# ELU with its exponential in the free half of h's PSUM bank, masks built in three steps, range check behind the last ELU

## The chip, the cores and the metric

The kernel runs on one core of one Trainium2 chip. The core has a matrix engine (TensorE, PE in the profile), a vector engine (VectorE, DVE), an activation engine (ScalarE, ACT), a general engine (GpSimd, POOL), and a queue engine (SyncE, SP) which here issues every transfer to 16 DMA engines. Each engine works through its own instructions in a fixed order and waits on semaphores for the others. The metric is the device time of one execution in microseconds. A profiled execution also has a span, from the first instruction to the last, which is a little shorter than its time.

## The reference

Attention with sink keys and a sliding window, then a two-layer network with an ELU between the layers:

```python
scores = scale * np.matmul(q, k.transpose(0, 1, 3, 2))       # 4 x 8 heads, 768 x 768, head_dim 64
keep = is_sink | in_window                                   # first n_sink=4 keys, or 0 <= rel < window=128
scores = np.where(keep, scores, -1000000000.0)
a = np.exp(scores - np.max(scores, axis=-1, keepdims=True))
x = np.matmul(a / (np.sum(a, axis=-1, keepdims=True) + 1e-09), v)
h = x @ w_in                                                 # 3072 x 512 by 512 x 2048
g = np.where(h > 0.0, h, alpha * (np.exp(np.minimum(h, 0.0)) - 1.0))
return (g @ w_out).astype(np.float32)                        # 2048 x 512
```

The weights come as 64-bit floats, everything else as 32-bit floats.

## The kernel before

The 24 tiles of 128 tokens are grouped into nine chunks of 2, 2, 2, 3, 3, 3, 3, 3 and 3 tiles (`SIZES`). For each chunk the attention goes through four pairs of heads, and in each pair through the chunk's tiles. Scores are made on PE (L540, L541, L547) into one of two PSUM banks `s`. DVE adds a mask and takes the row extreme (L566, one instruction for each head), ACT takes the exponential (L568), ACT and DVE write a high and a low half-precision part of the probabilities into `pq` (L580, L581), SP transposes `pq` into `pt` by DMA (L599), and PE multiplies by the values (L610, L615) into `po`, from which `x` is taken (L623, L624). There are three masks: `m0` for a sequence's first tile, `m1` for its second, `m2` for all others. `make_masks` builds `m0` and `m1` at once at the start, from `nw`, the two scalars that a DMA brings (`words`, L938 to L945), and returns `rest`, which builds `m2` and is an operation of the plan.

The feed-forward part takes 16 blocks of 128 hidden units, one after the other. A block `f` is 12 matmuls into one of two PSUM banks `h` (L651), the ELU, and three groups of matmuls into the accumulators `acc` (L672). The ELU is five operations: the exponential of `h` on ACT into the SBUF buffer `g` (L659), a subtraction and scaling of `g` in place on DVE (L661), the minimum with 0 and maximum with `h` on DVE (L662), a half-precision copy `gh` on ACT (L664), and the difference `gl` on POOL (L665). A bank holds 512 numbers a partition; a two-tile chunk uses 256 of them and a three-tile chunk 384. Chunks 0 and 1 go through the blocks in two halves each (`PARTS`), since the weights are still arriving: each of 32 weight pieces is loaded by SP (L395), put together from 64-bit words by one ACT and three DVE operations (L267 to L270), and split into two half-precision parts by ACT and POOL (L416, L417).

All of this is written as tasks of a `Plan`. PE's order is set by hand, by a position `pos`. The order on the other engines comes from a list scheduler: it gives each task a due time, counted back from PE's, and each engine takes, among the tasks that are ready by the plan's own costs (the second argument of `add`), the one that is due first. `keep_order` then writes the tasks in that order, and each engine keeps it. So a changed cost can move instructions on ACT, DVE, POOL and SP.

At the end `in_range` (L725 to L731) checks on DVE that the values stayed in range, a matmul with ones (L741) gathers this over the partitions, and `decide` (L735 to L737) makes a flag. Every engine loads the flag from SBUF (`TENSOR_LOAD`, L968) and jumps over a general path (L969) which isn't run here.

Of the kernel before, what the change touches and what calls it, by code (L numbers as in the profile page):

```python
# [280 lines left out]
def make_masks(nc, tmp, sk, nw, m0, m1, m2):  # L281
# [9 lines left out]
    nc.vector.tensor_scalar(sk, sk, nw[:, 0:1], None, ALU.is_lt)  # L291
# [7 lines left out]
    nc.vector.tensor_tensor(own, own, kp, ALU.mult)  # L299
# [4 lines left out]
    nc.gpsimd.memset(m0[:, 0:NS], MASKED)  # L304
# [1 line left out]
    for m in (m1, m2):
        nc.gpsimd.memset(m[:, KW : KW + NS], MASKED)
# [2 lines left out]
    nc.vector.tensor_copy(rel[:, 0:NS], kp[:, 0:NS])  # L310
    nc.vector.tensor_tensor(kp[:, 0:NS], kp[:, 0:NS], sk, ALU.max)
# [1 line left out]
    nc.gpsimd.memset(m1[:, 0:NS], MASKED)

    def rest():
        to_mask(m2[:, KW + NS : 2 * KW], own)
        nc.vector.tensor_copy(kp[:, 0:NS], rel[:, 0:NS])
        to_mask(m2[:, NS:KW], kp)
        to_mask(m2[:, 0:NS], sk)

    return rest


def fast_path(tc, ctx, first, kq, vx, wt, out, nw, flag):
# [672 lines left out]
```

## Time and profile before

| | before |
|---|---|
| time, median of 3 runs | 664.21 us (663.05 to 664.29) |
| time of the profiled execution | 662.14 us |
| its span | 660.3 us |
| busy share of the span: DVE, ACT, POOL | 69%, 69%, 51% |
| share of the chain that ended last: PE, DVE, ACT, POOL, DMA | 78%, 7%, 5%, 3%, 3% |
| mean granted PE clock | 0.984 |

The page gives busy times, and the chain of work that ended last, followed back from the last instruction. The tables by stretch of time give each engine's busy microseconds in a stretch, with the number of instructions in brackets, then the granted PE clock (1.00 is full), the DMA engines' busy share and the GB/s. In the tables of groups a row is a line, an engine, an operation and a form, then the count, the busy time and the mean ns of one, then the idle time of the engine ahead of these instructions and what ended it. In the order of time a row has the start, the length and the instruction, and in square brackets how long its engine was idle before it. An engine's name with a q behind it is its sequencer.

### The profile page before, as it was taken

To read this page: it belongs to the slowest core of one execution; us is meant where nothing else is said; L and a number is where in the kernel's file an instruction comes from. 1 tells how busy PE (TensorE), PEld (TensorE's weight loads), DVE (VectorE), ACT (ScalarE), POOL (GpSimd) and SP (SyncE) were. 2 spreads that over 40 slices of the span, in tenths; PEclk is the share of its full clock that TensorE was granted. 3 is DMA by queue.
4 is the path that set the end of the run, shared out by engine and by line. 5 is a ranking of instruction groups with operands and counts; after the bars stand their busy time and mean duration, and the time that the engine had idled before them with its cause. 6 is when DMAs were issued, how large, how long until landed. Compare 5 with 4: busy or idle time off the path is not lost.

```text
span 660.3 us, 13443 instructions
## 1 busy us (share of the span) xinstructions
PE 609.9 (92%) x4449; PEld 370.2 (56%) x4449; DVE 458.4 (69%) x1251; ACT 456.9 (69%) x1340; POOL 338.2 (51%) x497
## 2 busy tenths in 40 slices
PE   3486799789999999999999999999999999999996
PEld 2343466456776665555555556555555565555552
DVE  6999998896677776667677776758677787524222
ACT  4999786777788887767677777766677777523221
POOL 0158866785556666544555655444446564322221
PEclk9999698899999999999999999999999999999998
DMA  7989974857654586435454566555554734211001
GB/s 264 206 282 266 276 199 144 269 142 167 145 118 128 136 184 131 116 92 171 116 152 118 133 156 167 104 111 171 112 155 128 208 84 101 49 56 49 1 0 54
DMA packets 130110, 93.41 MB, mean 141 GB/s; under 512 B 104432, under 2 KB 109552, under 8 KB 130032
## 3 DMA queue, kind: packets, MB, share of 16 engines
q1 hardware_dynamic: 130032, 92.47, 53.2%
q8 instruction: 37, 0.61, 0.4%
q14 instruction: 41, 0.34, 0.2%
HBM read 59.94 MB, written 7.34 MB: 102 GB/s over the span
## 4 chain that ended last, share of the span: by engine, by line
PE 78%; DVE 7%; ACT 5%; issue 4%; POOL 3%; DMA 3%; SPq 0%; DVEq 0%; POOLq 0%; ACTq 0%
PE h L651 33%; PE acc L672 33%; PE po L610 5%; PE s L540 3%; PE s L541 3%; DMA pt<-pq 2%; PE s L547 1%; ACT e L568 1%; DVE wu L268 1%; POOL kq L487 1%; DVE wv L270 1%; DVE wu L269 1%; DVE pq L581 1%; DVE g L661 1%; POOL kq L489 1%
## 5 line engine op out<-in xcount | busy, mean ns | idle before, releaser
L651 PE MATMUL h<-x,w 128*128 128x384 f16 (+1 forms) x1728 | 276.6, 310 | 5.6 <-DVE g L662 5.6
L665 POOL TENSOR_TENSOR gl<-g,gh 128x384 f16<-128x384 f32 (+1 forms) x144 | 126.9, 882 | 215.2 <-ACT gh L664 184.4
L651 PEld LDWEIGHTS <-w 128*128 128x128 f16 x1728 | 165.6, 99 | 98.7 <-issue 5.9
L672 PE MATMUL acc<-w,gh 128*128 128x512 f16 x768 | 195.3, 384 | 0.8 <-DVE wv L693 0.8
L661 DVE TENSOR_SCALAR g<-g 128x384 f32<-128x384 f32 (+1 forms) x144 | 65.3, 454 | 115.8 <-ACT g L659 115.3
L659 ACT ACTIVATE g<-h 128x384 f32<-128x384 f32 (+1 forms) x144 | 64.9, 451 | 88.3 <-PE h L651 83.1
L581 DVE SCALAR_TENSOR_TENSOR pq<-e,st,pq 128x256 f16<-128x256 f32 (+1 forms) x192 | 107.2, 587 | 19.7 <-ACT pq L580 19.1
L672 PE MATMUL acc<-w,gl 128*128 128x512 f16 x384 | 110.6, 383 | 0.6 <-POOL gl L665 0.4
L672 PEld LDWEIGHTS <-gh 128*128 128x128 f16 x768 | 70.9, 98 | 71.5 <-issue 3.0
L568 ACT ACTIVATE e<-e,st 128x264 f32<-128x264 f32 (+1 forms) x192 | 93.4, 487 | 11.1 <-DVE st L566 9.7
L664 ACT ACTIVATE gh<-g 128x384 f16<-128x384 f32 (+1 forms) x144 | 69.3, 481 | 44.6 <-DVE g L662 44.2
L566 DVE CUSTOM_DVE_ANT_0 e<-s,m 128x264 f32<-128x264 f32 (+1 forms) x192 | 73.0, 404 | 32.1 <-PE s L541 26.8
L580 ACT ACTIVATE pq<-e,st 128x256 f16<-128x256 f32 (+1 forms) x192 | 85.1, 480 | 10.5 <-DVE st L573 10.1
L487 POOL TENSOR_TENSOR kq<-kqs,kq 128x396 fp32r<-128x396 f32 (+1 forms) x56 | 67.2, 1199 | 23.9 <-ACT kq L483 23.0
L662 DVE SCALAR_TENSOR_TENSOR g<-g,h 128x384 f32<-128x384 f32 (+1 forms) x144 | 72.6, 504 | 1.6
L672 PEld LDWEIGHTS <-gl 128*128 128x128 f16 x384 | 37.6, 99 | 47.9 <-POOL gl L665 2.5
L483 ACT ACTIVATE kq<-kqs 128x780 fp32r<-128x780 f32 (+2 forms) x56 | 48.4, 879 | 17.1 <-PE s L541 14.3
L417 POOL TENSOR_TENSOR w<-wv,w 128x512 f16<-128x512 f32 x32 | 39.5, 1236 | 38.8 <-ACT w L416 18.9
L489 POOL TENSOR_TENSOR kq<-kqs,kq 64x384 fp32r<-64x384 f32 (+1 forms) x56 | 56.7, 1013 | 4.4
L610 PE MATMUL po<-pt,vh 128*64 128x128 f16 x704 | 41.7, 230 | 17.8 <-DMA pt<-pq 7.8
L540 PE MATMUL s<-kq 128*128 128x264 f32 x160 | 56.2, 370 | 1.7 <-POOL kq L489 1.6
L610 PEld LDWEIGHTS <-vh 128*64 128x64 f16 x704 | 31.1, 115 | 29.6 <-issue 21.7
(78 smaller groups left out, 629.2 us busy)
## 6 DMA issues: line engine op xcount, KB each, us to landing
raw<-in_wt_dram SPq DMA_DIRECT2D x32, 512.0 KB, 5.6
kqs<-in_kq_dram SPq DMA_DIRECT2D x24, 456.0 KB, 3.4
kqs<-in_kq_dram SPq DMA_DIRECT2D x24, 390.0 KB, 3.3
out_dram<-wv SPq DMA_DIRECT2D x24, 256.0 KB, 2.5
vs<-in_vx_dram SPq DMA_DIRECT2D x20, 256.0 KB, 3.1
vm<-in_vx_dram SPq DMA_DIRECT2D x6, 768.0 KB, 4.6
kqs<-in_kq_dram SPq DMA_DIRECT2D x12, 326.0 KB, 4.1
vs<-in_vx_dram SPq DMA_DIRECT2D x12, 320.0 KB, 3.1
```

Of the source, the lines that this page charges most:

```text
L487: nc.gpsimd.tensor_tensor(buf[:, KQ_MAX : KQ_MAX + n] if c >= DUP else buf[:, kw : 2 * kw], raw[:, :n], hi[:, :n].bitcast(F32), ALU.subtract)
L540: nc.tensor.matmul(sp[:, :wd], q, hi[:, c0 : c0 + wd], start=True, stop=False)
L566: red = add("DVE", 0.13 + 0.00145 * wd, lambda ee=ee, me=me, sp=sps[e], m=m, wd=wd: nc.vector.tensor_tensor_reduce(ee, sp[:, :wd], m[:, :w ...
L568: ex = add("ACT", 0.48 + 0.00085 * wd, lambda ee=ee, me=me, rs=rs[:, e : e + 1]: nc.scalar.activation(ee, ee, AF.Exp, bias=me, scale=-1.0, ...
L580: a = add("ACT", act_us(nb * P, True), lambda src=src, hi=hi, re=re: nc.scalar.activation(hi, src, AF.Copy, scale=re), deps=[rr])
L581: b = add("DVE", dve_us(nb * P) + 0.1, lambda src=src, hi=hi, lo=lo, re=re: nc.vector.scalar_tensor_tensor(lo, src, re, hi, ALU.mult, ALU. ...
L610: nc.tensor.matmul(po[e * D : (e + 1) * D, oc], vv[:, vo : vo + D], pt[:, (2 * e + part) * nb + i, :], start=new, stop=last)
L651: nc.tensor.matmul(hp[:, :n], win[:, part, d, :], xx[:, :n], start=k == 0, stop=k == 3 * ND - 1)
L661: b = add("DVE", 0.1 + 0.0008 * n, lambda gf=gf: nc.vector.tensor_scalar(gf, gf, -1.0, G_SCALE, ALU.add, ALU.mult), deps=[a])
L662: b = add("DVE", dve_us(n), lambda gf=gf, hp=hp: nc.vector.scalar_tensor_tensor(gf, gf, 0.0, hp[:, :n], ALU.min, ALU.max), deps=[b])
L665: tl = add("POOL", pool_us(n), lambda gl=gl, gf=gf, gh=gh: nc.gpsimd.tensor_tensor(gl[:, :n], gf, gh[:, :n], ALU.subtract), deps=[th])
L672: nc.tensor.matmul(acc[i], gg[:, i * P : (i + 1) * P], wout[:, part, :], start=f == f0 and k == 0, stop=f == f1 - 1 and k == 2)
```

## The change

1. **ELU.** In chunks whose `h` uses at most half of its bank (chunks 0, 1 and 2: 48 of the 144 blocks), the exponential goes to the second half of the same bank, and the subtraction on DVE reads it there and writes `g` in SBUF. In three-tile chunks nothing moves.
2. **Masks.** `make_masks` is a generator. What needs no scalars stands ahead of them, `m0` follows at once, and `m1` and `m2` are operations of the plan (`mask1`, `mask2`). A product of two comparisons becomes one instruction, three copies go, and two four-column writes are added.
3. **Scalars.** The four comparisons and the reduction which test that `n_sink` and `window` are allowed become an operation of the plan (`allowed`) instead of standing ahead of the masks.
4. **Range check.** It also depends on the last block's L662, and its matmul stands behind PE's last accumulation instead of ahead of the last block's.
5. **Costs of the plan.** The exponential, the subtraction and POOL's split of the weights have other costs. `ON_ACT` is empty, so the weights' operations are the same.

```diff
 def make_masks(nc, tmp, sk, nw, m0, m1, m2):
...
     nc.vector.tensor_copy(rel, ri)
+    nc.vector.tensor_scalar(kp, rel, 0.0, None, ALU.is_ge)
...
+    for m in (m0, m1):
+        nc.gpsimd.memset(m[:, 0:NS], MASKED)
...
-    nc.vector.tensor_scalar(own, rel, nw[:, 1:2], None, ALU.is_lt)
-    nc.vector.tensor_scalar(kp, rel, 0.0, None, ALU.is_ge)
-    nc.vector.tensor_tensor(own, own, kp, ALU.mult)
-    nc.vector.tensor_copy(kp, own)
-    nc.vector.tensor_tensor(kp[:, 0:NS], kp[:, 0:NS], sk, ALU.max)
-    to_mask(m0[:, NS:KW], kp)
+    yield
+    nc.vector.tensor_scalar(sk, sk, nw[:, 0:1], None, ALU.is_lt)
+    nc.vector.scalar_tensor_tensor(own, rel, nw[:, 1:2], kp, ALU.is_lt, ALU.mult)
+    to_mask(m0[:, NS:KW], own)
+    nc.vector.tensor_tensor(kp[:, 0:NS], own[:, 0:NS], sk, ALU.max)
+    to_mask(m0[:, NS : 2 * NS], kp[:, 0:NS])
+    yield
     to_mask(m1[:, KW + NS : 2 * KW], own)
...
     nc.vector.tensor_scalar(kp, rel, float(P), nw[:, 1:2], ALU.add, ALU.is_lt)
-    nc.vector.tensor_copy(rel[:, 0:NS], kp[:, 0:NS])
-    nc.vector.tensor_tensor(kp[:, 0:NS], kp[:, 0:NS], sk, ALU.max)
     to_mask(m1[:, NS:KW], kp)
...
+    nc.vector.tensor_tensor(rel[:, 0:NS], kp[:, 0:NS], sk, ALU.max)
+    to_mask(m1[:, NS : 2 * NS], rel[:, 0:NS])
+    yield
+    to_mask(m2[:, KW + NS : 2 * KW], own)
+    to_mask(m2[:, NS:KW], kp)
+    to_mask(m2[:, 0:NS], sk)
+    yield
...
+    masks = make_masks(nc, tmp[:, : 4 * P], tmp[:, 4 * P : 4 * P + NS], nw, m0, m1, m2)
+    next(masks)
+    scalars()
+    next(masks)
...
-    rest_ = add("DVE", 0.9, rest)
+    mask1 = add("DVE", 1.0, lambda: next(masks))
+    mask2 = add("DVE", 0.6, lambda: next(masks), deps=[mask1])
+    allowed = add("DVE", 0.7, allowed)
...
-        tl = add("POOL", 1.5, lambda: nc.gpsimd.tensor_tensor(w[k][:, 1, :], v, w[k][:, 0, :], ALU.subtract), deps=[th])
+        tl = add("POOL", 1.22, lambda: nc.gpsimd.tensor_tensor(w[k][:, 1, :], v, w[k][:, 0, :], ALU.subtract), deps=[th])
...
-            a = add("ACT", act_us(n) + 0.06, lambda gf=gf, hp=hp, sums=sums: nc.scalar.activation(gf, hp[:, :n], AF.Exp, scale=1.0 / G_SCALE, accum_out=sums), deps=[s1])
+            ex = hp[:, n : 2 * n] if 2 * n <= 512 else gf
+            a = add("ACT", act_us(n) + 0.15, lambda ex=ex, hp=hp, sums=sums: nc.scalar.activation(ex, hp[:, :n], AF.Exp, scale=1.0 / G_SCALE, accum_out=sums), deps=[s1])
             exps_done.append(a)
-            b = add("DVE", 0.1 + 0.0008 * n, lambda gf=gf: nc.vector.tensor_scalar(gf, gf, -1.0, G_SCALE, ALU.add, ALU.mult), deps=[a])
+            b = add("DVE", 0.4 if 2 * n <= 512 else 0.45, lambda gf=gf, ex=ex: nc.vector.tensor_scalar(gf, ex, -1.0, G_SCALE, ALU.add, ALU.mult), deps=[a])
             b = add("DVE", dve_us(n), lambda gf=gf, hp=hp: nc.vector.scalar_tensor_tensor(gf, gf, 0.0, hp[:, :n], ALU.min, ALU.max), deps=[b])
             ring("h", [s1], [b])
+            g_done.append(b)
...
-    a = add("DVE", 2.0, in_range, deps=seen + exps_done)
-    b = add("PE", 0.1, lambda: nc.tensor.matmul(sp[:, 0:3], ones, some16, start=True, stop=True), deps=[a], pos=start + 2 * LAG - 1.5)
+    a = add("DVE", 2.0, in_range, deps=seen + exps_done + g_done[-1:] + [allowed])
+    b = add("PE", 0.1, lambda: nc.tensor.matmul(sp[:, 0:3], ones, some16, start=True, stop=True), deps=[a], pos=start + 2 * LAG)
```

PE's order is the same in the whole fast path, except for the check's matmul. On the other engines most of the order up to the third chunk differs in places. Three places matter below.

DVE at the start, from the scalars to the first masked scores (L566 before, L576 now, whose mask is the last name; `pt` is scratch space here, `m_172`, `m_173`, `m_174` before and `m_163`, `m_164`, `m_165` now are `m0`, `m1`, `m2`). Before, the last of 20 rows that stand between the scalars and the scores:

```order
L294 TENSOR_SCALAR m_173<-pt_108 128x128
L294 TENSOR_SCALAR m_174<-pt_108 128x128
L302 TENSOR_TENSOR pt_108<-pt_108 128x4
L294 TENSOR_SCALAR m_172<-pt_108 128x128
L309 TENSOR_SCALAR pt_108<-pt_108,words 128x128
L310 COPY pt_108<-pt_108 128x4
L311 TENSOR_TENSOR pt_108<-pt_108 128x4
L294 TENSOR_SCALAR m_173<-pt_108 128x128
L317 COPY pt_108<-pt_108 128x4
L294 TENSOR_SCALAR m_174<-pt_108 128x128
L294 TENSOR_SCALAR m_174<-pt_108 128x4
L566 ISA e_91,st_94<-s_166,m_172 128x132
```

Now, where ten rows stand there, the last of them:

```order
L303 TENSOR_SCALAR m_164<-pt_99 128x128
L303 TENSOR_SCALAR m_163<-pt_99 128x4
L317 TENSOR_SCALAR pt_99<-pt_99,words 128x128
L303 TENSOR_SCALAR m_164<-pt_99 128x128
L319 TENSOR_TENSOR pt_99<-pt_99 128x4
L303 TENSOR_SCALAR m_164<-pt_99 128x4
L576 ISA e_82,st_85<-s_157,m_163 128x132
L576 ISA st_85 128x1
L576 ISA e_82,st_85<-s_158,m_163 128x132
L576 ISA st_85 128x1
L303 TENSOR_SCALAR m_165<-pt_99 128x128 x2
L303 TENSOR_SCALAR m_165<-pt_99 128x4
```

The five operations of `allowed` and the three writes of `m2` no longer stand ahead of the first scores. `m2` is written right behind the first pair of them, and `allowed` stands some 300 rows further on.

DVE at the first block's ELU (`h` in PSUM, `g` in SBUF). Before:

```order
L573 RECIPROCAL st_96<-st_96 128x2
L661 TENSOR_SCALAR g_109<-g_109 128x256
L270 SCALAR_TENSOR_TENSOR wv_121<-acc_171,wu_125 128x512
L566 ISA e_92,st_98<-s_166,m_174 128x264
L566 ISA st_98 128x1
```

Now:

```order
L583 RECIPROCAL st_87<-st_87 128x2
L673 TENSOR_SCALAR g_100<-h_155 128x256
L271 TENSOR_SCALAR wu_115<-raw_117 128x512
L576 ISA e_83,st_89<-s_157,m_165 128x264
L576 ISA st_89 128x1
```

The source of the subtraction is now `h`'s bank, and another piece of the weights' work stands behind it.

DVE at the end, from the last block's subtraction to the jump (`checks` and `some` belong to the range check, `wv` is a tile of the result). Before:

```order
L729 TENSOR_REDUCE some<-checks 128x1
L730 TENSOR_SCALAR some<-some 128x2
L731 CAST some_204<-some 128x3
L662 SCALAR_TENSOR_TENSOR g_110<-g_110,h_165 128x384
L735 TENSOR_REDUCE some<-s_166 128x1
L736 TENSOR_SCALAR some<-some 128x1
L737 TENSOR_TENSOR words<-words,some 128x1
L967 CAST words<-words 128x1
L697 TENSOR_SCALAR wv_121<-acc_169 128x512
L697 TENSOR_SCALAR wv_123<-acc_171 128x512
L968 TENSOR_LOAD words
L969 COMPARE_AND_BRANCH
```

Now:

```order
L744 CAST some_193<-some 128x3
L710 TENSOR_SCALAR wv_112<-acc_160 128x512
L710 TENSOR_SCALAR wv_114<-acc_162 128x512
L748 TENSOR_REDUCE some<-s_157 128x1
L749 TENSOR_SCALAR some<-some 128x1
L750 TENSOR_TENSOR words<-words,some 128x1
L985 CAST words<-words 128x1
L986 TENSOR_LOAD words
L987 COMPARE_AND_BRANCH
```

The check's seven operations stand behind the last ELU instead of inside it, and the flag is made behind the last tiles of the result instead of ahead of them.

More of the change, by code (lines that the diff above doesn't have):

```diff
@@ L48 @@
 DUP = 2
+ON_ACT = ()
 AHEAD = 5
@@ L254, in dma_us, with weight_f32 @@
     return nbytes / 330e3
-def weight_f32(nc, v, d, u, raw):
+def weight_f32(nc, v, d, u, raw, on_act=False):
     ui = u.bitcast(U16).rearrange("p (f t) -> p f t", t=2)
@@ L270, in weight_f32 @@
         lambda: nc.vector.scalar_tensor_tensor(v.bitcast(I32), d.bitcast(I32), 3, u, ALU.logical_shift_left, ALU.bitwise_or),
-    )
+    ]
+    if on_act:
+        steps[1] = lambda: nc.scalar.activation(ui[:, :, 0], halves[:, :, 1], AF.Copy, scale=2.0**-13, bias=-4095.5 / 8192)
+    return steps
 def elu(nc, g, h, scale):
@@ L287, in make_masks, with fast_path @@
     nc.vector.tensor_copy(rel, ri)
+    nc.vector.tensor_scalar(kp, rel, 0.0, None, ALU.is_ge)
     for j in range(NS):
         nc.gpsimd.memset(sk[:, j : j + 1], float(j))
[L291 removed]
+    for m in (m0, m1):
+        nc.gpsimd.memset(m[:, 0:NS], MASKED)
+    for m in (m1, m2):
+        nc.gpsimd.memset(m[:, KW : KW + NS], MASKED)
     def to_mask(dst, keep):
         nc.vector.tensor_scalar(dst, keep, -1.0, -MASKED, ALU.add, ALU.mult)
[L297 to L304 removed]
+    yield
[5 more added lines that the diff above has]
+    yield
     to_mask(m1[:, KW + NS : 2 * KW], own)
[L306 to L307 removed]
     nc.vector.tensor_scalar(kp, rel, float(P), nw[:, 1:2], ALU.add, ALU.is_lt)
[L310 to L311 removed]
     to_mask(m1[:, NS:KW], kp)
[L313 to L324, printed above, removed]
+    nc.vector.tensor_tensor(rel[:, 0:NS], kp[:, 0:NS], sk, ALU.max)
[5 more added lines that the diff above has]
+    yield
+def fast_path(tc, ctx, first, kq, vx, wt, out, nw, flag, scalars, allowed):
     nc = tc.nc
@@ L399, in step @@
         def step(i):
-            return lambda: weight_f32(nc, v, acc[2], wu[k % RINGS["wu"]], raw)[i]()
+            return lambda: weight_f32(nc, v, acc[2], wu[k % RINGS["wu"]], raw, k in ON_ACT)[i]()
         ld = add("SP", 0.4, load, deps=[w_done.get(k - AHEAD, [None])[0]], lat=dma_us(P * 512 * 8))
@@ L404, in weights @@
             a = add("ACT", act_us(512), step(0), deps=[ld])
-            u1 = add("DVE", 0.65, step(1), deps=[ld])
+            u1 = add("ACT", act_us(512), step(1), deps=[ld]) if k in ON_ACT else add("DVE", 0.65, step(1), deps=[ld])
             u2 = add("DVE", 0.7, step(2), deps=[ld])
@@ L964, in attention_moe @@
         with ExitStack() as inner:
-            fast_path(tc, inner, first, kq, vx, wt, out, nw, f[:, 0:1])
+            fast_path(tc, inner, first, kq, vx, wt, out, nw, f[:, 0:1], scalars, allowed)
         nc.vector.tensor_copy(flag, f[:, 0:1])
```

31 lines of the change are left out of this document (16 added, 15 removed).

## The prediction

> **What bounds the kernel now.** I read the busy times first, then the table by stretches of time.
>
> ```profile
> PE 609.9 (92%) x4449; PEld 370.2 (56%) x4449; DVE 458.4 (69%) x1251; ACT 456.9 (69%) x1340; POOL 338.2 (51%) x497
> 20.00:40.00 20.00, 13.18 (x118) 8.93 (x116) 19.14 (x61) 17.95 (x56) 5.22 (x7) 1.00 0.96 269
> 40.00:60.00 20.00, 15.48 (x136) 9.44 (x135) 19.28 (x56) 19.61 (x62) 13.52 (x22) 1.00 0.97 271
> 60.00:80.00 20.00, 12.30 (x92) 7.99 (x90) 20.00 (x42) 15.04 (x40) 16.54 (x23) 0.74 0.92 241
> 80.00:100.00 20.00, 17.88 (x144) 12.51 (x144) 18.74 (x43) 17.85 (x53) 14.69 (x20) 1.00 0.78 216
> 100.00:120.00 20.00, 18.46 (x126) 12.35 (x126) 16.62 (x38) 14.17 (x39) 13.71 (x20) 0.91 0.53 157
> 120.00:140.00 20.00, 15.95 (x116) 9.87 (x115) 17.28 (x37) 15.57 (x42) 15.35 (x16) 0.91 0.65 208
> 140.00:160.00 20.00, 17.11 (x137) 11.87 (x135) 15.04 (x42) 14.14 (x44) 13.50 (x22) 1.00 0.70 164
> 200.00:220.00 20.00, 19.50 (x161) 13.82 (x159) 14.60 (x47) 16.97 (x56) 12.45 (x18) 1.00 0.58 139
> ```
>
> PE is busy 609.9 of 660.3 us, so 50.4 us of the span are PE's idle time. The seven stretches from 20 to 160 us hold 29.6 of them, and in the stretch 200 to 220 PE already works 19.50 of 20 us. From 20 to 100 us DVE works 19.14 + 19.28 + 20.00 + 18.74 = 77.2 of 80 us: DVE is the bound there. From 100 to 160 it works 48.9 of 60 us and is no longer the bound alone. So a microsecond taken from DVE ahead of 100 us should arrive at the end, if PE is really late for that reason; one taken later arrives in part; one taken behind 200 us is worth nothing. And whatever the tail gains or loses counts in full.
>
> **The start.** In order of time on DVE, the times at which the instructions start:
>
> ```profile
> 6.25 0.15 DVE L948 TENSOR_SCALAR words<-words 128x1 f32<-128x1 f32 x1
> 6.50 0.22 DVE L291 TENSOR_SCALAR pt<-pt,words 128x4 f32<-128x4 f32 x1
> 6.82 0.15 DVE L952 TENSOR_REDUCE words<-words 128x1 f32<-128x4 f32 x1
> 6.94 0.29 DVE L299 TENSOR_TENSOR pt<-pt 128x128 f32<-128x128 f32 x1
> 7.41 0.35 DVE L294 TENSOR_SCALAR m<-pt 128x128 bf16<-128x128 f32 x2
> 8.45 0.17 DVE L310 COPY pt<-pt 128x4 f32<-128x4 f32 x1
> 8.65 0.16 DVE L311 TENSOR_TENSOR pt<-pt 128x4 f32<-128x4 f32 x1
> 9.11 0.17 DVE L317 COPY pt<-pt 128x4 f32<-128x4 f32 x1
> 9.53 0.29 DVE L566 CUSTOM_DVE_ANT_0 e<-s,m 128x132 f32<-128x132 f32 x1
> 11.27 0.43 DVE L566 CUSTOM_DVE_ANT_0 e<-s,m 128x264 f32<-128x264 f32 x1 [0.76 <-PE s L547]
> ```
>
> The first masked scores start at 9.53, and the whole pipeline hangs on them. What leaves the stretch ahead of them, by the distance from each start to the next: four comparisons 6.50 − 6.25 = 0.25, the reduction 6.94 − 6.82 = 0.12, the product L299 and the copy behind it 7.41 − 6.94 = 0.47, the copy L310 0.20, and L317 with the writes of `m2` 9.53 − 9.11 = 0.42. Together 1.46 us. Two four-column writes come in; starts of such small instructions lie 0.07 to 0.20 apart, so I take 0.13 each: **−1.2 us** (−1.3 to −1.06). The writes of `m2`, about 0.4 us, now follow the first scores, under the 0.76 us for which DVE waits for PE ahead of the second pair; without that gap they would cost these 0.4. `allowed` (0.4 us, the 0.25 and 0.12) goes to about 130 us, where DVE has 2.7 us free in 20; packed tight it would cost 0.4.
>
> **The ELU of chunks 0 to 2.** First L661's group in 40 to 100 us and in 100 to 160 us, then L661 and L662 with minimum, median and maximum, then a form that reads PSUM, the first and the last of five long L661 in 40 to 100 us, and a group of the weights in 100 to 160 us:
>
> ```profile
> L661 DVE TENSOR_SCALAR g<-g 128x256 f32<-128x256 f32 x13 | 7.3, 564 | 0.6 <-ACT g L659 0.6
> L661 DVE TENSOR_SCALAR g<-g 128x256 f32<-128x256 f32 x16 | 9.4, 593 | 5.3 <-ACT g L659 5.1
> L661 DVE TENSOR_SCALAR g<-g x49: 267/295/1244, 38.0 to 226.6; 128x256 f32<-128x256 f32 x48, 128x384 f32<-128x384 f32 x1
> L662 DVE SCALAR_TENSOR_TENSOR g<-g,h x48: 396/412/422, 40.3 to 222.3; 128x256 f32<-128x256 f32 x48
> L624 DVE SCALAR_TENSOR_TENSOR x<-po,x 128x256 f16<-128x256 f32 x12 | 4.9, 409 | 0.0
> 44.95 1.24 DVE L661 TENSOR_SCALAR g<-g 128x256 f32<-128x256 f32 x1
> 99.07 1.10 DVE L661 TENSOR_SCALAR g<-g 128x256 f32<-128x256 f32 x1
> L269 DVE TENSOR_SCALAR wu<-raw 128x512 uint16<-128x512 uint16 x10 | 7.2, 720 | 2.7 <-DMA raw<-in_wt_dram 2.7
> ```
>
> L661 has two prices: 0.27 to 0.30 us, or up to 1.24. L662, which has one operand in PSUM, is never stretched (396 to 422 ns) although it writes the same SBUF buffer. So an SBUF-to-SBUF subtraction sometimes waits inside its own time, and one that reads PSUM should not. The change makes L661 such an instruction, of the same size: I take 0.41 us, that of L624 and L662. In the DVE-bound stretch that is 13 × (0.564 − 0.41) = −2.0 us, if the waits vanish. They may move on instead: L269 reads and writes SBUF too, and may take them over. Were each wait W beyond 0.41 us to pass to the next instruction, a stretched L661 would save only 0.28 and an unstretched one cost 0.13: with five long ones of the 13, one at 0.42 and seven short ones that is −5 × 0.28 + 7 × 0.13 = −0.5 us. I take **−1.3 us** between the two. From 100 to 160 us 16 × (0.593 − 0.41) = 2.9 us of DVE work go, under engines that aren't full; **−0.5 us** (0 to −2).
>
> The wait for the stretched ones is where a rule of the skill bears. The Trainium skill (SBUF — State Buffer, SBUF: two separate sides) says that VectorE in its two-port modes, or with two SBUF inputs, and GpSimd take a shared pair of ports as an exclusive lock for a whole instruction. By it all waits leave L661, and the stage gains the full 2.0 us unless the next instruction wants the lock; the rows of L661 and L662 fit it.
>
> The exponential on ACT writes PSUM instead of SBUF. The nearest rows:
>
> ```profile
> L267 ACT ACTIVATE acc<-raw 128x512 f32<-128x512 f32 x32 | 20.2, 630 | 2.2 <-DVE wv L270 1.3 <-DMA raw<-in_wt_dram 0.7
> L416 ACT ACTIVATE w<-wv 128x512 f16<-128x512 f32 x32 | 19.9, 621 | 0.7 <-DVE wv L270 0.5
> ACT g L659 <- POOL gl L665: 0.7, 1, 0.7
> ```
>
> L267 writes PSUM at 630 ns, L416 writes SBUF at 621 ns: 0.01 us × 48, either sign, and ACT has 2 us or more free in all stretches shown but one. Nothing. The wait for `g` to be free (POOL and ACT of two blocks earlier) moves from ACT's exponential to DVE's subtraction; behind it on DVE stand scores and weights. On ACT this wait came once and cost 0.7 us (the last row), so I put it at 0 with an end of +0.7.
>
> **The end.** In order of time, and the sequencers' rows of the flag's load (L968) and of the jump (L969):
>
> ```profile
> 652.16 0.16 DVE L735 TENSOR_REDUCE some<-s 128x1 f32<-128x3 f32 x1 [1.14 <-PE s L741]
> 652.67 0.10 PEld L672 LDWEIGHTS <-gl 128*128 128x128 f16 x1 [0.62 <-POOL gl L665]
> 654.40 0.69 DVE L697 TENSOR_SCALAR wv<-acc 128x512 f32<-128x512 f32 x1 [0.60 <-PE acc L672]
> L968 PEldq TENSOR_LOAD <-words x1: 482/482/482, 652.9 to 652.9; - x1
> L969 PEldq COMPARE_BRANCH  x1: 3944/3944/3944, 653.5 to 653.5; - x1
> L969 DVEq COMPARE_BRANCH  x1: 72/72/72, 655.3 to 655.3; - x1
> L969 DVEq EVENT_SEMAPHORE  x1: 21/21/21, 658.8 to 658.8; - x1
> ```
>
> Without the check inside the last ELU PE's weight load needn't wait 0.62 us for `gl`. I count half of it, 0.3 us, since the matmuls ahead were still running in that time (0 to 0.6). So the last tile is evacuated at 655.09 − 0.3 = 654.8. But the flag, now made behind it, takes from 652.16 to 652.9 = 0.7 us, so it is there at 655.5 instead of 652.9, and every engine's load (0.48) and jump waits for it. PE jumps at 656.0 instead of 653.5, and its jump took 3.94 us: to 659.9. DVE jumps at 656.1; from its jump to its next instruction 3.5 us passed: 659.6. Before, the latest of the two was DVE's 658.8. So the end moves by about **+0.8 us**: 0 if these jumps take only 658.8 − 656.1 = 2.7 us where the stores no longer run beside them, +1.4 if PE's wait gives nothing back.
>
> That jumps are dear agrees with the Trainium skill (Runtime: NRT & Kernel Launch, Instruction fetch mechanics), which says that a taken branch out of the fetched window stalls for a fetch.
>
> **The moved order.** On ACT, DVE, POOL and SP the tasks are re-sorted up to the third chunk. The work is the same, PE's order too, and at the marks that I compared (each tile of `x`, each block's subtraction, each fourth weight piece) DVE has mostly the same work ahead of them or one weight piece less. I take 0. Its ends are what one such collision costs:
>
> ```profile
> PE po L610 <- DMA pt<-pq: 7.8, 6, 2.5
> 101.23 2.67 PE acc L672 x6
> 107.85 1.29 PE acc L672 x6
> ```
>
> PE waited up to 2.5 us for a transpose, and behind such a wait the same six matmuls took 2.67 instead of 1.29 us, in stretches whose granted clock is 0.91. One more or one less: ±(2.5 + 1.4) = ±3.9 us.
>
> **The sum.** −1.2 − 1.3 − 0.5 + 0.8 + 0 = −2.2 us on the profiled execution's 662.14 us: 659.9. The median of the runs shown is 664.21, 2.1 us above that execution, so the same step gives **662.0 us** as the median to expect. Its own range is that of the four terms' ends, of which all four won't come together: half of the way to −5.3 gives 660.4, and half of the way to +0.5 (−1.06 − 0.5 + 0 + 1.4 + 0.7) gives 663.4.
>
> **The rivals.**
> - *The gain is taken back ahead of 160 us*, because transfers bind: the DMA engines are busy 0.92 to 0.97 from 20 to 80 us. Against it: DVE's only wait for a load in 20 to 160 us is L269's 2.7 us, behind 100 us. Then half of the start's gain and nothing of the ELU's arrives: −0.6 + 0.8 = +0.2, 664.4. Chance 0.20.
> - *A collision more*: the re-sorted SP queue puts a transpose behind a load near 95 or 118 us, PE idles, and its clock drops. It decides from the point where a `pq` part is later than the gap that PE has ahead of its values. −2.2 + 3.9 = +1.7: 665.9, slower. Chance 0.15.
> - *A collision less*: −2.2 − 3.9 = −6.1: 658.1. Chance 0.12.
> - *PSUM is only dearer*: the waits stay and each subtraction costs 0.41 − 0.28 = 0.13 more, 13 of them in the bound stretch: −1.2 + 1.7 + 0.8 = +1.3: 665.5. The Trainium skill (VectorE: DVE Perf Modes, Rules for kernel authors) speaks for it, since a PSUM source runs at the single rate. L662's 396 to 422 ns speak against the waits. Chance 0.05.
> - The forecast: 0.48.
>
> **How the numbers follow.** About 0.2%, 1.33 us, is what a measurement of this kernel can tell from no change. The forecast and a collision less are faster, transfers that bind are no change, a collision more and a dearer PSUM are slower; but some of the forecast's own range lies within 1.33 us of 664.21: faster 0.56, within 0.24, slower 0.20. The range leaves out the far side of the two collision cases: 658.4 to 665.8.
>
> **What would show it.** The first L566 at 8.3 instead of 9.53. L661 of the 256 form between 0.40 and 0.43 us throughout, with L268, L269 and L581 no longer than before on average; if they grow by what L661 loses, the waits moved on. DVE less than full in 80 to 100 us, and PE's idle sum ahead of 160 us some 3 us smaller. At the end no wait for `gl`, the flag's load near 3 us nearer to the end, and 0.8 us more from the last matmul's end to the end of the span. The forecast is wrong if PE's waits for `pt` grow, or if slow stretches of PE's clock come or go.

## The result, and the profile after

| | before | after |
|---|---|---|
| time, median | 663.63 us (4 runs, 661.84 to 664.29) | 673.46 us (4 runs, 671.47 to 674.69) |
| profiled execution, its span | 662.14, 660.3 us | 673.48, 671.7 us |
| mean granted PE clock | 0.984 | 0.976 |

The ratio is 1.015 (95% interval 1.0117 to 1.0182): slower by 7.8 to 12.1 us, where the prediction had 662.0 and a range up to 665.8. Of after, the busy times, three stretches of the table by time, and PE's waits ahead of 160 us (us in total, times, longest):

```profile
PE 614.8 (92%) x4449; PEld 372.5 (55%) x4449; DVE 463.1 (69%) x1249; ACT 456.5 (68%) x1340; POOL 333.2 (50%) x497
60.00:80.00 20.00, 11.79 (x93) 7.78 (x88) 19.55 (x40) 16.52 (x43) 16.29 (x26) 0.82 0.81 255
80.00:100.00 20.00, 13.86 (x93) 8.79 (x92) 12.62 (x31) 10.96 (x31) 8.33 (x12) 0.66 0.75 177
240.00:260.00 20.00, 17.47 (x133) 10.21 (x132) 13.52 (x34) 15.10 (x44) 12.32 (x21) 1.00 0.65 150
PE po L620 <- DMA pt<-pq: 11.4, 7, 3.5
PE h L661 <- POOL w L427: 6.2, 5, 2.1
```

PE's busy time has grown by 4.9 us although its matmuls are the same, so its clock was lower; its idle time has grown by 671.7 − 614.8 − 50.4 = 6.5 us. From 80 to 100 us PE does 13.86 us of work, where it did 17.88, at a clock of 0.66 instead of 1.00. DVE is busy for 63% and ACT for 55% of this stretch, and PE's only wait of note in it is for `pt`, 6.1 us: DVE is no longer what PE waits for there. Ahead of 160 us the waits for `pt` are 11.4 us instead of 7.8. PE's matmuls also wait 6.2 us for the weights' low part `w` from POOL; in before only a weight load waited for it, once, 2.2 us.

Where the time went is best seen as a lag: the start of the ELU's last DVE operation (minimum and maximum, L662 before) in the k-th of the 144 blocks, minus that of before. I worked it out from the rows in order of time of each profiled execution; the last column is the difference of the spans. A positive lag means that the run is behind before. Each row is one execution, and the 29 executions of before that were timed beside `e1` lie between 659.1 and 665.6 us. So steps of several microseconds count, and small differences between rows don't.

| lag in us at block (us in before) | 5 (70) | 10 (88) | 29 (158) | 52 (239) | 60 (275) | end of span |
|---|---|---|---|---|---|---|
| after | 0.5 | 9.4 | 5.9 | 7.0 | 9.9 | 11.4 |
| `e1_exp_alone` | -0.1 | 1.2 | -3.6 | -4.1 | -4.2 | -3.5 |
| `e2_order_alone` | -1.0 | 6.0 | 6.7 | 7.6 | 12.1 | 13.2 |
| `e3_tail_alone` | -0.1 | 1.0 | -0.3 | -0.3 | -0.3 | 1.1 |
| `e4_all_old_costs` | 1.6 | 5.6 | 1.6 | 1.0 | 1.0 | 2.4 |
| `e5_costs_alone` | 1.1 | 5.1 | 6.5 | 7.4 | 9.5 | 10.2 |
| `e8_order_kept` | -1.0 | 0.4 | -3.6 | -4.2 | -4.2 | -3.3 |
| `e13_four_loads_behind` | -0.9 | 2.4 | 0.6 | 2.3 | 5.2 | 6.5 |
| `e16_new_then_old` | -1.3 | 7.9 | 3.5 | 2.9 | 2.9 | 4.1 |
| `e17_both_pairs` | -2.0 | 1.4 | -0.4 | 1.5 | 1.6 | 3.0 |
| `e18_order_kept_one_move` | -1.7 | -2.1 | -0.9 | -1.5 | -1.5 | -0.6 |

The changed kernel loses 9 us between 70 and 88 us, gets 3.5 back, and loses 2.8 more at 243 us; from block 60 on nothing happens until the tail. The first loss in order of time, on SP's sequencer and then on PE:

```profile
76.05 0.33 SPq L492 DMA_DIRECT2D kqs<-in_kq_dram  x1
76.47 0.38 SPq L405 DMA_DIRECT2D raw<-in_wt_dram  x1
77.03 0.33 SPq L517 DMA_DIRECT2D vs<-in_vx_dram  x1
77.88 1.25 SPq L609 DMA_TRANSPOSE pt<-pq  x1
79.18 0.58 SPq L405 DMA_DIRECT2D raw<-in_wt_dram  x1
80.03 3.02 SPq L609 DMA_TRANSPOSE pt<-pq  x1
84.07 0.42 PE L620 MATMUL po<-pt,vh 128*64 128x128 f16 x4 [3.49 <-DMA pt<-pq]
87.67 0.42 PE L620 MATMUL po<-pt,vh 128*64 128x128 f16 x4 [2.65 <-DMA pt<-pq]
88.56 1.89 PE L685 MATMUL acc<-w,gh 128*128 128x512 f16 x4
```

Four loads (326 + 512 + 256 + 512 KB by the page's table of transfers) are issued ahead of and between two transposes, which land 6.1 and 7.6 us after their issue; over the whole execution the median is 2.9. Each lands 1.0 to 1.3 us behind the load ahead of it: at 84.03 and 87.63, the loads at 82.78 and 86.64. PE waits twice, and the four matmuls behind the second wait take 1.89 us, where 1.03 is usual.

### The profile page after: what moved, and what is told of

It reads as the page before. It is cut to its first block, busy times and chain, and to the rows that moved or that the text cites. A ratio compares the mean times of both kernels' runs of the same rounds, so it can differ in the third digit from the quotient of the medians.

```text
span 671.7 us, 13438 instructions
## 1 busy us (share of the span) xinstructions
PE 614.8 (92%) x4449; PEld 372.5 (55%) x4449; DVE 463.1 (69%) x1249; ACT 456.5 (68%) x1340; POOL 333.2 (50%) x497
## 4 chain that ended last, share of the span: by engine, by line
PE 74%; DVE 9%; DMA 6%; ACT 4%; POOL 3%; issue 3%; SPq 1%; DVEq 0%; POOLq 0%; ACTq 0%
PE acc L685 32%; PE h L661 32%; PE po L620 4%; DMA pt<-pq 4%; PE s L550 3%; PE s L551 2%; DVE pq L591 2%; DMA raw<-in_wt_dram 2%; DVE wv L273 1%; DVE wu L272 1%; DVE wu L271 1%; POOL kq L497 1%; DVE e L576 1%; ACT pq L590 1%; POOL kq L499 1%
## 5 line engine op out<-in xcount | busy, mean ns | idle before, releaser
L661 PE MATMUL h<-x,w 128*128 128x384 f16 (+1 forms) x1728 | 281.6, 313 | 11.8 <-POOL w L427 6.2
L661 PEld LDWEIGHTS <-w 128*128 128x128 f16 x1728 | 166.8, 99 | 107.8 <-POOL w L427 10.1
L591 DVE SCALAR_TENSOR_TENSOR pq<-e,st,pq 128x256 f16<-128x256 f32 (+1 forms) x192 | 113.5, 617 | 19.6 <-ACT pq L590 18.6
L673 DVE TENSOR_SCALAR g<-g 128x384 f32<-128x384 f32 x96 | 43.4, 452 | 99.5 <-ACT g L671 99.1
L671 ACT ACTIVATE g<-h 128x384 f32<-128x384 f32 x96 | 47.0, 489 | 76.5 <-PE h L661 74.1
L576 DVE CUSTOM_DVE_ANT_0 e<-s,m 128x264 f32<-128x264 f32 (+1 forms) x192 | 72.0, 404 | 35.0 <-PE s L551 28.5
L427 POOL TENSOR_TENSOR w<-wv,w 128x512 f16<-128x512 f32 x32 | 39.3, 1231 | 45.5 <-ACT w L426 45.3
```

What stands on the lines that cost most here:

```text
L576: red = add("DVE", 0.13 + 0.00145 * wd, lambda ee=ee, me=me, sp=sps[e], m=m, wd=wd: nc.vector.tensor_tensor_reduce(ee, sp[:, :wd], m[:, :w ...
L591: b = add("DVE", dve_us(nb * P) + 0.1, lambda src=src, hi=hi, lo=lo, re=re: nc.vector.scalar_tensor_tensor(lo, src, re, hi, ALU.mult, ALU. ...
L661: nc.tensor.matmul(hp[:, :n], win[:, part, d, :], xx[:, :n], start=k == 0, stop=k == 3 * ND - 1)
```

## Experiments: the parts apart

**`e1_exp_alone`.** Before, with the exponential in `h`'s bank. The plan's costs stay, so the order on each engine does too.

```diff
-            a = add("ACT", act_us(n) + 0.06, lambda gf=gf, ...: nc.scalar.activation(gf, hp[:, :n], AF.Exp, ...
+            ex = hp[:, n : 2 * n] if 2 * n <= 512 else gf
+            a = add("ACT", act_us(n) + 0.06, lambda ex=ex, ...: nc.scalar.activation(ex, hp[:, :n], AF.Exp, ...
```

> The kernel before with the exponential of chunks 0 to 2 in the free half of h's bank, and nothing else: the plan's costs, and so the order on every engine, stay those of before. Theory O (the 10 us come from the re-sorted order, the operations are at worst neutral): between 660.5 and 664.5, L661's 256 form at 0.40 to 0.43 us. Rival P (the operations themselves are dearer: the subtraction has lost its fast mode, the wait for g stands on DVE): at least +3, so 666.5 or more, with DVE's waits for gl showing in 40 to 160 us.

659.69 us against 663.0, ratio 0.9949 (0.9928 to 0.9969): faster, a little below what theory O had. Rival P, dearer operations, falls. The groups of DVE's instructions from 0 to 240 us, first of before, then of this run:

```profile
L581 DVE SCALAR_TENSOR_TENSOR pq<-e,st,pq 128x256 f16<-128x256 f32 x64 | 37.1, 611 | 5.6 <-ACT pq L580 5.5
L661 DVE TENSOR_SCALAR g<-g 128x256 f32<-128x256 f32 x48 | 23.8, 497 | 12.8 <-ACT g L659 12.6
L269 DVE TENSOR_SCALAR wu<-raw 128x512 uint16<-128x512 uint16 x32 | 22.6, 707 | 2.8 <-DMA raw<-in_wt_dram 2.7
L268 DVE TENSOR_SCALAR wu<-raw 128x512 uint16<-128x512 uint16 x32 | 20.9, 654 | 0.0
```

```profile
L581 DVE SCALAR_TENSOR_TENSOR pq<-e,st,pq 128x256 f16<-128x256 f32 x64 | 38.9, 640 | 6.1 <-ACT pq L580 6.0
L269 DVE TENSOR_SCALAR wu<-raw 128x512 uint16<-128x512 uint16 x32 | 24.0, 748 | 0.2
L268 DVE TENSOR_SCALAR wu<-raw 128x512 uint16<-128x512 uint16 x32 | 22.2, 694 | 0.0
L662 DVE TENSOR_SCALAR g<-h 128x256 f32<-128x256 f32 x48 | 19.9, 416 | 12.8 <-ACT h L660 8.5 <-POOL gl L666 2.5 <-POOL kq L487 1.0
```

The subtraction (L661, here L662) loses 3.9 us; the three others, whose operations didn't change, gain 1.8 + 1.4 + 1.3 = 4.5. In this order the waits moved on completely, and DVE has no less to do. The lag shows where the gain comes from: it is +1.6 at block 14 (100 us), −1.8 at block 17 (113 us) and −2.4 at block 21 (134 us). PE there, first before, then this run:

```profile
100.32 0.37 PE L610 MATMUL po<-pt,vh 128*64 128x128 f16 x4 [2.19 <-DMA pt<-pq]
101.16 1.89 PE L672 MATMUL acc<-w,gh 128*128 128x512 f16 x4
123.66 0.30 PE L610 MATMUL po<-pt,vh 128*64 128x128 f16 x4 [2.53 <-DMA pt<-pq]
124.17 1.79 PE L672 MATMUL acc<-w,gh 128*128 128x512 f16 x4
```

```profile
100.91 0.30 PE L610 MATMUL po<-pt,vh 128*64 128x128 f16 x4 [0.92 <-DMA pt<-pq]
101.42 1.04 PE L673 MATMUL acc<-w,gh 128*128 128x512 f16 x4
121.55 0.30 PE L610 MATMUL po<-pt,vh 128*64 128x128 f16 x4 [1.54 <-DMA pt<-pq]
122.06 1.04 PE L673 MATMUL acc<-w,gh 128*128 128x512 f16 x4
```

Two waits for a transpose are shorter by 1.3 and 1.0 us, and PE's clock doesn't fall behind them. So the gain is not DVE's time; it appears where these two waits are shorter. That the two waits make it is argued from one execution of each and not shown. Other runs speak against so simple a reading: in `e14` below the wait near 100 us is 0.84 us and the clock from 100 to 105 us is 1.00, but the next wait, at 123.87, is 3.92 us and the lag is +0.2 afterwards; in `e8` PE waits 3.63 us at 121.15 and the lag is −3.6 at block 29 all the same.

**`e2_order_alone`.** The changed kernel, with the exponential and the subtraction in place in `g` again; the costs and the order are the changed kernel's.

```diff
-            ex = hp[:, n : 2 * n] if 2 * n <= 512 else gf
+            ex = gf
```

> The changed kernel with the exponential and the subtraction in place in g, as before, while the plan's costs and the order on every engine stay those of the changed kernel. O: it is as slow as the changed kernel, 672 to 675, with PE waiting for transposes at 80 to 88 us as there. P: it is faster than the changed kernel by what the operations cost, 664 to 668.

674.85 against 663.0, ratio 1.0181 (1.0153 to 1.021). The loss is there without the new operations in the ELU: theory O.

**`e3_tail_alone`.** Before, with the range check behind the last ELU (`g_done`, and the position of its matmul, as in the change).

> The kernel before with the range check behind the last ELU and its matmul behind the last accumulation, nothing else. From the lag of the two profiled executions, 9.87 us at the last ELU and 11.4 at the end of the span: +1.5, so 665.1 (the prediction's working gave +0.8: 664.4). Rival: the jumps cost the same wherever they stand and the matmul's wait is regained: 663.6, no change.

663.66 against 663.0, ratio 1.0023 (1.0004 to 1.0041): 0.3 to 2.7 us slower. This doesn't tell the rival's 663.6 from 664.4 and 665.1; in the trace the lag grows by 1.4 us behind block 60. The sequencers' rows of the flag's load, three of after's five, and of PE's jump:

```profile
L986 SPq TENSOR_LOAD <-words x1: 737/737/737, 665.3 to 665.3; - x1
L986 DVEq TENSOR_LOAD <-words x1: 817/817/817, 665.3 to 665.3; - x1
L986 PEldq TENSOR_LOAD <-words x1: 753/753/753, 665.3 to 665.3; - x1
L987 PEldq COMPARE_BRANCH  x1: 3884/3884/3884, 666.2 to 666.2; - x1
```

All five engines now load the flag at once, where in before three did and two came 0.8 and 1.5 us later. PE's load takes 0.75 us instead of 0.48. Its jump takes 3.88 us, and took 3.94.

**`e4_all_old_costs`.** The changed kernel with the three old costs.

```diff
-        tl = add("POOL", 1.22, ...
+        tl = add("POOL", 1.5, ...
-            a = add("ACT", act_us(n) + 0.15, ...
+            a = add("ACT", act_us(n) + 0.06, ...
-            b = add("DVE", 0.4 if 2 * n <= 512 else 0.45, ...
+            b = add("DVE", 0.1 + 0.0008 * n, ...
```

> The changed kernel with the plan's three costs as before: exp +0.06, subtraction 0.1 + 0.0008 n, POOL's split 1.5. O, with the costs as what re-sorts: the start's gain of 1.2 and the ELU's 1 to 2 arrive, the tail costs 1.5: 661 to 664.5. Rival M (it is the masks' new place in the plan that re-sorts): 670 or more. P: 668 or more.

663.36 against 663.0, ratio 0.9999 (0.9978 to 1.0021). So the masks' place in the plan (rival M) doesn't bring the loss, and dearer operations (P) don't either.

**`e5_costs_alone`** (before with the three new costs: the edit above the other way round) **and `e6_masks_alone`** (the change's masks, `scalars` and `allowed` with all else as before).

> The kernel before with the plan's three new costs and nothing else: the operations are those of before, the order on ACT, DVE, POOL and SP is sorted anew. Theory C (the new costs make the bad order): 670 or more, with PE waiting for the split weights and for transposes between 70 and 95 us. Rival M (the masks' and the scalars' place in the plan makes it, the costs are harmless): 665 or less. Rival B (it takes both): in between.

> The kernel before with the masks and the scalars in steps of the plan, nothing else (old costs, exponential in g, range check where it was). The first masked scores start 1.2 earlier in every theory. C: 662 to 664.5 (the start arrives, or is lost again). M: 668 or more. From the kernel with all parts and old costs, 663.4, whose exponential gives 3.4 and whose tail takes 1.5, one gets 663.4 + 3.4 - 1.5 = 665.3, if the parts add up.

The costs alone take 671.74 against 662.99, ratio 1.0127 (1.0092 to 1.0162); the masks alone 663.47, ratio 1.0018 (0.9998 to 1.0038), as theory C had it, but without the start's gain. Three numbers that no instruction on the chip contains bring nearly the whole loss. The lag of `e5` steps up at the same two places, by 4.0 us at the first instead of 8.9.

The collision near 80 us alone doesn't decide the time. PE's wait for the first of the pair in `e4`, then in `e5`:

```profile
83.80 0.30 PE L620 MATMUL po<-pt,vh 128*64 128x128 f16 x4 [3.54 <-DMA pt<-pq]
82.76 0.42 PE L610 MATMUL po<-pt,vh 128*64 128x128 f16 x4 [3.60 <-DMA pt<-pq]
```

The waits are the same, and so nearly are the lags at block 10, 5.6 and 5.1. Behind it `e4` wins 4.6 us back by block 60, and `e5` loses 4.4 more. Their operations differ too, so this isn't the order alone.

**`e9_cost_pool`, `e10_cost_exp`, `e11_cost_subtraction`.** Before, with one of the three new costs each.

> The kernel before, where only the plan's cost of POOL's split of the weights is new: 1.22 instead of 1.5. The three new costs together took 663.0 to 671.7. Theory A (the costs add up, each shifts the order a little its own way): the three single ones sum to about +8.7. Theory D (each re-sorted order is a draw of its own, what decides is which probabilities and weights come late in it): the three don't add up, each lies somewhere between 659 and 676. This one moves the least on the engines: A +1, so 664; D says no number.

> The kernel before, where only the plan's cost of the exponential is new: 0.15 over ACT's usual cost instead of 0.06. A: +3, so 666; D: anywhere between 659 and 676, and not the third that is left to add up to 671.7.

> The kernel before, where only the plan's cost of the subtraction is new: 0.4 or 0.45 instead of 0.1 + 0.0008 n. It moves as much as the three together do on the engines. A: +5, so 668; D: anywhere between 659 and 676.

670.17, 667.17 and 666.25 against 662.75; ratios 1.0111 (1.0079 to 1.0143), 1.0063 (1.0042 to 1.0084), 1.0056 (1.0038 to 1.0075). They sum to 15.3 us where all three together cost 8.7: they don't add up, as theory D has it. All lie above before, though, so the results aren't spread around it either. Late landings aren't needed for an early loss: in `e10` the two transposes land in 3.1 and 2.8 us, and the lag at block 10 is 5.1; they are issued 3.7 and 3.2 us later than in before.

## Experiments: by what the order costs

**`e7_sp_of_old_costs`.** The changed kernel; the plan is solved twice, with the new and the old costs, and SP takes the second order, the others the first.

```diff
+        line = {e: [t for t in (old if e in OLD else new) if t.eng == e] for e in self.HOP}
```

> The changed kernel, where SP alone has the order that the old costs give, while ACT, DVE, POOL and PE keep the changed kernel's. Theory S (the loss is SP's queue: transposes behind loads): 666 or less, and no transpose near 80 us that takes 7 us to land. Rival W (the loss is in the order of ACT, DVE and POOL, where the weights come late and the probabilities too): 671 to 676, PE's waits for w and pt as in the changed kernel.

681.0 against 662.99, ratio 1.0273 (1.0239 to 1.0306). Worse than either: an order of SP that doesn't fit the others' holds up more (PE waits 7.2 us for one transpose behind 180 us). Theory S as put, that SP's whole queue is to blame, falls; but W's number is missed too.

**`e12_load_behind_transpose` and `e13_four_loads_behind`.** The changed kernel with loads moved behind transposes on SP's queue and nothing else: the one of 79.18 us, then all four shown above, behind the pair.

```diff
+    after, n = queue[nth[15]], 0
+    for t in [queue[i] for i in range(nth[14] - 3, nth[15]) if i not in nth]:
...
+        tasks.remove(t)
+        to = tasks.index(after) + 1 + n
...
+            tasks.insert(to, t)
+            n += 1
```

> The changed kernel, where one instruction of SP is moved: the load of a weight piece that it issues at 79.18 us stands behind the transpose of 80.03 instead of ahead of it. Theory T (the transpose takes 7.6 us to land because 512 KB stand ahead of it in the queues): it lands in 3 to 4 us, PE's two waits at 84 and 88 us shrink by about 4, and the time goes to 668 to 670. Rival W (the probabilities and the weights come late there whatever SP does, a later weight gives it back): 672 to 674.

> The changed kernel, where SP issues four loads (the keys and values at 76.05 and 77.03, two weight pieces at 76.47 and 79.18) behind the pair of transposes instead of ahead of them. T: both transposes land in 3 to 4 us instead of 6.1 and 7.6, PE's waits at 84 and 88 us go down from 6.1 to 2 or less, and the lag behind the kernel before at 95 us goes from 9.2 to about 4; at the end 667 to 670. W: the waits move to the scores or to the weights, 672 to 675.

One load: 671.78 against 662.75, ratio 1.0124 (1.0092 to 1.0157). The transposes still take 5.8 and 6.8 us, with the three other loads ahead of them; the median gains less than T said, though the interval (668.9 to 673.2) reaches into both theories' ranges. Four loads: 668.65 against 663.53, ratio 1.0087 (1.0062 to 1.0111), as T said. SP and PE there:

```profile
76.64 3.82 SPq L609 DMA_TRANSPOSE pt<-pq  x2
80.56 0.52 SPq L492 DMA_DIRECT2D kqs<-in_kq_dram  x1
81.12 0.43 SPq L405 DMA_DIRECT2D raw<-in_wt_dram  x1
81.07 0.30 PE L620 MATMUL po<-pt,vh 128*64 128x128 f16 x4 [2.14 <-DMA pt<-pq]
81.86 0.42 PE L620 MATMUL po<-pt,vh 128*64 128x128 f16 x4 [0.21 <-DMA pt<-pq]
```

The transposes land in 3.0 to 4.4 us, PE's two waits go from 6.1 to 2.35 us, and the lag at block 10 from 9.4 to 2.4. The two weight pieces land 3.6 and 1.0 us later than in after, which fits PE's waits for `w`, 7.3 instead of 6.2 us.

**`e17_both_pairs`.** The same, and at 242 us too. There, in after:

```profile
238.79 0.52 SPq L517 DMA_DIRECT2D vs<-in_vx_dram  x1
239.36 2.14 SPq L711 DMA_DIRECT2D out_dram<-wv  x2
241.60 0.37 SPq L492 DMA_DIRECT2D kqs<-in_kq_dram  x1
242.07 6.21 SPq L609 DMA_TRANSPOSE pt<-pq  x2
247.88 0.30 PE L620 MATMUL po<-pt,vh 128*64 128x128 f16 x4 [2.53 <-DMA pt<-pq]
```

> As the run with four loads behind the pair at 78 us, and at 242 us the load of values, the two stores and the load of keys also behind the transpose that they stand ahead of. T: that transpose lands in 3 us instead of 5.8, PE's wait of 2.5 us there goes, and the lag's step of 2.8 at 243 us with it: 668.7 - 2.5 = 666, between 665 and 667. W: the step stays, 668 to 669.5.

665.32 against 663.05, ratio 1.0043 (1.0025 to 1.0061). The transpose lands in 2.9 us, PE has no wait there, and the second step of the lag is gone. Eight transfers moved on one queue bring the 9.8 us over before down to 2.3. That isn't the whole price of the order: the same operations in the order of before take 658.0 (`e8` below), without the later range check, which cost 0.3 to 2.7 (`e3`). If these add up, some 4.5 to 7 us of the order's price lie elsewhere, and no run here shows where.

**`e14_extra_load_ahead` and `e15_extra_load_behind`.** The reverse, in the kernel before: a load of 768 KB into `vm`, that nothing reads, ahead of or behind the pair of transposes at 75 us.

```diff
+    at = tasks.index(queue[nth[14]]) + 0
+    tasks[at:at] = more
```

> The kernel before with one extra load of 768 KB (values, into a buffer that is not used until much later) on SP's queue ahead of the pair of transposes at 75 us; nothing reads it. T: the transposes land in 5 to 6 us instead of 2.9 to 3.6, PE waits some 2 us more at 79 us and its clock falls longer, lag at 95 us +3 to +5; at the end 665 to 668. W: within 1 us of the same load behind the pair.

> The same extra load behind the pair of transposes. T: the transposes land as before, 2.9 to 3.6 us; the loads of keys and weights behind it come up to 2.8 us later, which they have to spare: 662.5 to 664.5. W: within 1 us of the run with the load ahead.

Ahead 664.47, ratio 1.0015 (0.9993 to 1.0036); behind 663.33, ratio 0.9993 (0.997 to 1.0017). The transposes answer as T said: 5.0 and 5.8 us to land with the load ahead, 2.9 and 3.8 with it behind. The time doesn't: the intervals overlap. PE waits 4.20 us for the pair with the load ahead, but 2.07 + 1.07 with it behind, where the pair was issued 0.9 and 1.7 us later, and at block 10 the lags are 2.0 and 2.4. So the landing follows from what stands ahead, shown from both sides; its price in time is shown by `e13` and `e17` alone, and W isn't refuted here.

**`e16_new_then_old`.** The changed kernel's order up to the ninth exponential of the ELU, then the one of the old costs.

> The changed kernel, with its order up to the ninth exponential of the ELU (about 90 us) and from there on the order that the old costs give for what is left. H (the loss ahead of 95 us is what remains): lag 9 at 95 us and 671 to 674 at the end. Rival L (the loss is won back where the later order leaves room, as it is with the old costs throughout, from 5.6 at 95 us to 1.0 at the end): 664 to 668.

666.27 against 663.53, ratio 1.0047 (1.0025 to 1.007). The lag of 7.9 at block 10 is down to 2.9 at the end: rival L. So an early collision isn't lost for good; the new order's later part fails to win it back, and adds the one at 242 us.

**`e8_order_kept` and `e18_order_kept_one_move`.** A version from these results: the exponential in `h`'s bank and the short start, with the old costs, and `mask1` and `allowed` hung on tasks that were there, so that the order of before stays; the range check stands where it was. `e18` also moves four transfers behind the transpose of 115 us.

```diff
+    mask1 = None
+    mask2 = add("DVE", 0.9, lambda: next(masks))
+    steps = {"mask1": lambda: next(masks), "allowed": allowed}
...
+                    red = add("DVE", 0.13 + 0.00145 * wd, lambda ...: (nc.vector.tensor_tensor_reduce(...), steps.pop("mask1", int)() if last else None), ...
```

> The exponential in h's bank and the short start (m0 and m1 ahead of the scores as now, m2 behind the first pair, the test of the scalars behind the weights), in the order of before on every engine, with the old costs and the range check where it was. If the start's 1.2 us and the exponential's 3.4 add up: 658.4, and never above 661. If the timing near 100 us decides and the start shifts it back into the wait for the transpose: 662 to 663.

> The version in the order of before (exponential in h's bank, short start; 658.0), with two weight pieces and two stores moved behind the transpose of 115 us, which takes 5.8 us to land there. T: it lands in 3 to 4 us, PE's wait of 3.6 us at 121 shrinks to 1.5, and its slow clock behind it comes later or not at all: 655 to 657. Rival W: the two weight pieces that come later give it back: 658 to 660.

`e8`: 658.03 against 662.99, ratio 0.9928 (0.9906 to 0.9949): it beats both kernels. `e18`: 660.9 against 663.05, ratio 0.9969 (0.9953 to 0.9986): slower than `e8`, so T falls, and it gives back a little more than W said. The transpose lands in 2.9 us there, but two rows, of ACT and of PE, show what took its place:

```profile
123.03 0.66 ACT L270 ACTIVATE acc<-raw 128x512 f32<-128x512 f32 x1 [6.17 <-DMA raw<-in_wt_dram]
124.07 1.32 PE L685 MATMUL acc<-w,gh 128*128 128x512 f16 x4 [4.06 <-ACT gh L677]
```

ACT waits 6.17 us for a weight piece, one of the two moved ones, which lands at 122.95. It was itself about to be needed.

## Why the prediction was wrong

**The step that failed** is the moved order: "I take 0. Its ends are what one such collision costs", ±3.9 us. With before's operations in the ELU the changed order is 12 us slower (`e2`), and the plan's costs alone bring 8.7 (`e5`). I compared how much work stands ahead of certain marks on DVE. That is the wrong measure: the work was the same, but on SP four loads had come to stand ahead of two transposes, and nothing on DVE shows this. The rival *a collision more* named the mechanism, transposes behind loads, idle PE and a lower clock, and was right in it. It was priced as one collision with one wait and given 0.15. It expected the place near 95 or 118 us. There were three late transposes, two near 80 us and one at 242, with waits of 3.49, 2.65 and 2.53 us, and a later order that won back less (`e16`, and `e4` beside `e5`). Moving the transfers behind these transposes brought the time from 673.5 to 665.3 (`e17`). The prediction's own sign of being wrong showed it: PE's waits for `pt` grew from 7.8 to 11.4 us, and its clock in 80 to 100 us fell from 1.00 to 0.66.

**The start, −1.2 us:** right, and a little small. DVE's first masked scores, in order of time:

```profile
7.99 0.17 DVE L303 TENSOR_SCALAR m<-pt 128x4 bf16<-128x4 f32 x1
8.12 0.30 DVE L576 CUSTOM_DVE_ANT_0 e<-s,m 128x132 f32<-128x132 f32 x1
```

They start at 8.12 instead of 9.53, 1.41 us earlier, where the range ended at 1.3, and where the order is kept the gain is alive at block 5 (−1.0 in `e8`). At the end it can't be told for certain from the exponential's: `e8` and `e1` have the same lag of −4.2, and their gains over before, 4.8 and 3.4 us by the ratios, have intervals that overlap.

**The ELU, −1.3 us:** the size of L661 was right, the reason for a gain wrong. L661's line in after, by forms (minimum, median and maximum in ns):

```profile
L673 DVE TENSOR_SCALAR g<-g x96: 344/360/1390, 233.7 to 658.8; 128x384 f32<-128x384 f32 x96
L673 DVE TENSOR_SCALAR g<-h x48: 401/424/426, 38.6 to 228.8; 128x256 f32<-128x256 f32 x48
```

The 256 form takes 0.40 to 0.43 us throughout, as forecast. But the −1.3 lay between waits that vanish and waits that all move on, and in before's order they all moved on (`e1`: −3.9 on it, +4.5 on L268, L269 and L581). In the changed order they didn't: from `e2` to after, from 0 to 245 us, the subtraction loses 4.6 us and the same three groups (there L271, L272 and L591) gain 1.5. So what becomes of the waits depends on the order too. What the stretched ones wait for can be read from the trace of before, here a split of the weights on POOL and the L661 beside it:

```profile
44.84 1.19 POOL L417 TENSOR_TENSOR w<-wv,w 128x512 f16<-128x512 f32 x1 [0.99 <-ACT w L416]
44.95 1.24 DVE L661 TENSOR_SCALAR g<-g 128x256 f32<-128x256 f32 x1
```

Of before's 48 L661 of the 256 form, 18 take longer than 0.33 us. All 18 start while an instruction of POOL runs, and end 0.15 us after that instruction ends. The rule of the Trainium skill on the shared ports (SBUF — State Buffer, SBUF: two separate sides) agrees with these 18, with the narrow 401 to 426 ns of the form that reads PSUM, and with waits that go to the next instruction that wants the lock. The full −2.0 us that it would have allowed didn't come in `e1`'s first 100 us, where the lag is +1.2 at block 10. The 3.4 us that `e1` gained appear behind 100 us, where PE's two waits are shorter: I had such a term only as the rival *a collision less*, and that the waits are its cause stays open. *PSUM is only dearer* fell with `e1`.

**ACT at 0, and the wait for `g`:** right. L671 of this form takes 363 ns, L659 took 375; in `e1` DVE waits 2.5 us for POOL's `gl` ahead of the subtraction, its idle time there is 12.8 us as in before, and the kernel is faster.

**The end, +0.8 us:** inside what `e3` measured (0.3 to 2.7). Its working had a slip: of its own two ends, PE's 659.9 and DVE's 659.6, the later is PE's, so it should have said +1.1. The flag is ready at 665.27, which with the lag of 9.87 taken off is 655.4, where I had 655.5; PE's load then takes 0.27 us more than I counted.

**100 to 160 us, −0.5 us:** it can't be told apart beside the rest. **Transfers that bind**, the rival at 0.20, named the right resource; but it forecast a gain taken back, no loss, and most of the loss went when the same bytes were issued in another order (`e17`).

One marker misled: "DVE less than full in 80 to 100 us" came true, 12.62 of 20 us, because PE had stalled.

**Still open:** why all the new costs give worse orders. By the trace they are the truer ones (POOL's split 1231 ns on average, planned 1.22 instead of 1.5). That the old ones fit the transfers better by chance was not tried. Open too is the part of the order's price that isn't at the two places, and what makes the early loss of `e10`, whose transposes land in time.

## What to carry to other kernels

Where costs in a plan change along with operations, time the two apart: the new operations in the old order, and the old operations in the new one. Read the queue that issues transfers like any engine, and look at the loads that stand ahead of a short transfer on which the matrix engine waits and have not landed when it is issued; but move a load back only where its own user has time. A wait taken from one instruction is a gain only if the next doesn't inherit it, so compare the sum over all instructions that could.
